# Second MLP of a fused attention and MoE kernel: sums of the next tokens' blocks pinned on VectorE, four low parts moved there from GpSimd

## The chip, the core and the metric

The kernel runs on one core of one Trainium2 chip, in one launch. The metric is the device time of a launch in microseconds (us), lower is better. A time stated for a kernel is the median of several runs.

## The reference, cut to what matters

Attention over packed keys feeds a gated MLP, whose result (4608 tokens by 512) feeds a second MLP. The change touches the second MLP alone:

```python
def _moe2_ref(x, w_in, w_out):               # x 4608x512, w_in 512x2048, w_out 2048x512
    h = x @ w_in
    g = h * (1.0 / (1.0 + np.exp(-1.702 * h)))
    return (g @ w_out).astype(np.float32)
```

## The kernel before, in words

The second MLP starts at about 899 us of the 1638 us span. It reads `x` as the first MLP left it in DRAM.

**Tokens and groups.** Tokens are taken in five spans: three of 2x512 tokens, then two of 2x384. Each span runs four turns (groups of hidden units; `turns` lists span and group). Both matrix products are done on 2x2 blocks with seven products in place of eight, so that sums and differences of blocks are needed: of the tokens (`t1` to `t4`, beside the blocks `b11`, `b12`, `b21`, `b22`), of the hidden values and of the weights. Every factor is split into a high part (rounded by ScalarE) and a low part (the rest, by a subtraction), and each product is three matmuls: high by high, high by low, low by high.

**Steps.** `main` runs a loop over steps `c`. `up(c)` issues six matmuls of a product with the input weights (`ps_up`, L1065) and what reads its bank of PSUM: VectorE adds (L1078, L1080, L1085, L1087) and ScalarE's activation (L1088). A turn has 14 such steps, seven products for each of two halves `a`. `form(d)` makes one of seven factors for the product with the output weights: sums on VectorE (L1101 to L1103, L1105), the high part `oh` on ScalarE (L1109), the low part `ol` on GpSimd (L1110). `down(d)` issues the matmuls (`ps_dn`, L1136) and VectorE's additions to `accu` and `acc` (L1163, L1167). Each `down` uses one of two pairs of PSUM banks in alternation, and each `up` one of four banks, so TensorE waits where VectorE has not yet read a bank that comes round again.

**The next span's tokens.** `load_x` fetches the blocks of the next span, `sums(s, q)` makes their sums on VectorE in three calls: `t1` (L1024), `t3` (L1026) and `t2` (L1030, two instructions). In the program these stand in the span before the one that they serve, at steps 10 and 13 of its third turn and at step 2 of its fourth (`EARLY`). `prepare(s, q)` later splits each block into its two parts (L1041, L1042), in the last half of the fourth turn, and there also subtracts L1045.

**Order.** The program is recorded and a scheduler with a model of the engines' times then picks the order in which each engine's instructions stand. It may put an instruction ahead of others that the program has before it. Each engine then runs its own list strictly in that order. `tc.keep_in_program_order(i)` takes this freedom from one instruction.

Of the kernel before, what the change touches and what calls it, by code (L numbers as in the profile page):

```python
# [26 lines left out]
def fl(t):  # L27

    return t.bitcast(F32)
# [3 lines left out]
def tile_pack_attention__then__two_mlps(  # L33
# [14 lines left out]
    nc = tc.nc  # L48
# [782 lines left out]
    def mlp2(cv):  # L831
# [92 lines left out]
        def load_part(dst, i0, at0, n):  # L924
            end = at0 + n
            while at0 < end:
                b, s0 = divmod(at0, S)
                m = min(end - at0, S - s0)
                o = at0 + n - end
                nc.sync.dma_start(dst[:, :, o : o + m], x2_d[b][:, i0 : i0 + 2, s0 : s0 + m])  # L930
                at0 += m
# [55 lines left out]
        def main(wp, sp, pm, pa, later):  # L987
            turns = [(s, g) for s in range(len(spans)) for g in range(NGR)]
# [15 lines left out]
            xr = {}  # L1004

            def load_x(s):
                if s < len(spans):
                    t0, n = spans[s]
                    for q, i0, k in (("b11", 0, 0), ("b12", 0, 1), ("b22", 2, 1), ("b21", 2, 0)):
# [4 lines left out]
                        xr[q] = t[:, :, :n]  # L1014
                        load_part(xr[q], i0, t0 + k * n, n)

            def sums(s, q):

                if s == len(spans):
                    return  # L1020
                n = spans[s][1]
                if q == "t1":
                    xr[q] = wp.tile([P, 2, TH], F32, tag="xt", name="xr", bufs=1)[:, :, :n]
                    nc.vector.tensor_sub(xr[q], xr["b12"], xr["b11"])  # L1024
                elif q == "t3":
                    nc.vector.tensor_sub(xr["b12"], xr["b22"], xr["b12"])  # L1026
                else:
                    xr[q] = [cv.tile([P, TH], F32, tag="w", name="xr", bufs=2)[:, :n] for _ in range(2)]
                    for k in range(2):
                        nc.vector.tensor_sub(xr[q][k], xr["b22"][:, k], xr["t1"][:, k])  # L1030

            def prepare(s, q):

# [58 lines left out]
            def form(d):  # L1092

                t, j = divmod(d, 7)
                n = spans[turns[t][0]][1]
                a11, a12, a21, a22 = (g[t, z] for z in ((0, 0), (1, 0), (0, 1), (1, 1)))
                q = down_order[j][0]
                if q == "s2":
                    x = sp.tile([P, 2, TH], F32, tag="s1", name="s1", bufs=1)[:, :, :n]
                    g[t, "s1"] = x  # L1100
                    nc.vector.tensor_add(x, a21, a22)  # L1101
                    nc.vector.tensor_sub(a21, a11, a21)
                    nc.vector.tensor_sub(a11, x, a11)  # L1103
                elif q == "s4":
                    nc.vector.tensor_sub(a12, a12, a11)  # L1105
                source = {"a11": a11, "s2": a11, "a12": a12, "s4": a12, "s3": a21, "a22": a22}
                src = g[t, "s1"] if q == "s1" else source[q]
                oh, ol = (sp.tile([P, 2, TH], F32R, tag=f"o{x}", name=f"o{x}", bufs=3)[:, :, :n] for x in "hl")
                nc.scalar.copy(oh, src)  # L1109
                nc.gpsimd.tensor_sub(ol, src, fl(oh))  # L1110
                formed[d] = oh, ol

            acc, banks = {}, {}
# [68 lines left out]
            for d in range(7 * len(turns)):  # L1182
                t, j = divmod(d, 7)
# [3 lines left out]
            for c in range(len(ups) + PER + LAG):  # L1187
                if c < len(ups):
                    up(c)
                    load_wi(c + WIB)  # L1190
                    if c >= 7:
                        next(later, None)
                    s, at = turns[ups[c][0]][0], (turns[ups[c][0]][1] - NGR + 2) * PER + c % PER
                    if at == 6:
                        load_x(s + 1)
                    elif at in EARLY:
                        sums(s + 1, EARLY[at])
                for d in form_at.get(c, ()):
                    form(d)
                for d in down_at.get(c, ()):  # L1200
                    down(d)
                    load_wo(d + WOB)
# [167 lines left out]
```

## Time and profile before

| what | value |
|---|---|
| median of 3 runs | 1644.51 us (1642.76 to 1645.05) |
| the profiled execution | 1639.52 us, its span 1637.7 us |
| TensorE (PE) busy | 1599.6 us, 98% of the span |
| VectorE (DVE) busy | 1098.9 us, 67% |
| GpSimd (POOL) busy | 927.6 us, 57% |
| ScalarE (ACT) busy | 872.0 us, 53% |

The span runs from the first to the last instruction of the core; the profiled execution has 1.8 us around it. PE's busy time is that of matmuls, whose ends are modelled. Below, POOL is GpSimd and DVE is VectorE, as the profile's rows call them.

### The profile page before, as it was taken

The page shows a single profiled execution, that of the slowest core. Times are in us where ns is not written, and L with a number is a line of the kernel's source. Part 1 is how long each engine was busy: PE and PEld are TensorE (multiplying, and loading weights), DVE is VectorE, ACT ScalarE, POOL GpSimd, SP SyncE. Part 2 cuts the span into 40 slices and gives each one's busy share as a digit, 9 for nine tenths or more (in the row PEclk, how much of TensorE's full clock was granted, in tenths as well). Part 3 has the DMA queues.
Part 4 walks back from the last instruction along what each step waited for, and adds up shares of the span by engine and source line. Part 5 has one row for each costly group of instructions (what it writes and reads, how often), then busy time and mean ns, then how long its engine had stood idle before and what let it go on. Part 6 is the DMA issues. An engine that isn't in the chain of part 4 may idle for free.

```text
span 1637.7 us, 29088 instructions
## 1 busy us (share of the span) xinstructions
PE 1599.6 (98%) x10608; PEld 1514.1 (92%) x10608; DVE 1098.9 (67%) x1895; ACT 872.0 (53%) x1799; POOL 927.6 (57%) x753
## 2 busy tenths in 40 slices
PE   8999999999999999999999999899989999999997
PEld 5699999999999999999999899799979999999997
DVE  5777777767777777676764676844584458567466
ACT  5677777666566665565654544344343434434432
POOL 3547877656665566554655475554455445646444
PEclk9999999999999999999999999999999999999999
DMA  9756665866546655484544996576657667887874
GB/s 263 220 170 190 212 203 193 275 198 213 202 161 217 194 170 169 158 309 148 176 172 174 317 326 195 189 242 190 182 189 237 192 191 225 284 252 247 285 232 141
DMA packets 217725, 348.21 MB, mean 213 GB/s; under 512 B 93936, under 2 KB 123632, under 8 KB 211440
## 3 DMA queue, kind: packets, MB, share of 16 engines
q1 hardware_dynamic: 217584, 346.35, 66.0%
q8 instruction: 85, 1.39, 0.4%
q14 instruction: 56, 0.46, 0.1%
HBM read 279.19 MB, written 67.11 MB: 211 GB/s over the span
## 4 chain that ended last, share of the span: by engine, by line
PE 90%; DVE 5%; issue 1%; DMA 1%; ACT 1%; POOL 0%; SPq 0%; POOLq 0%; DVEq 0%; ACTq 0%
PE ps_dn L1136 20%; PE ps_up L1065 19%; PE ps_o L748 19%; PE ps_g L712 18%; PE ps_w L679 4%; PE ps_at L308 3%; PE ps_at L297 3%; PE ps_at L353 2%; PE ps_at L443 2%; DVE xr L1030 1%; PE ps_at L341 1%; DVE x_t L1042 1%; DMA xr<-x 1%; DVE xr L1045 0%; PE ps_at L281 0%
## 5 line engine op out<-in xcount | busy, mean ns | idle before, releaser
L1110 POOL TENSOR_TENSOR ol<-g,oh 128x1024 fp32r<-128x1024 f32 (+1 forms) x120 | 269.4, 2255 | 301.0 <-ACT oh L1109 300.1
L1136 PE MATMUL ps_dn<-wo,oh 128*128 128x256 f32 x2016 | 368.8, 284 | 9.7 <-DVE accu L1163 5.8
L1136 PEld LDWEIGHTS ps_dn<-wo,oh 128*128 128x128 f32 x2016 | 320.5, 192 | 17.4 <-DVE accu L1163 6.2
L748 PE MATMUL ps_o<-Hh,wo 128*128 128x384 f32 x1152 | 320.3, 340 | 0.1
L1136 PE MATMUL ps_dn<-wo,ol 128*128 128x256 f32 x1008 | 280.7, 284 | 1.0 <-POOL ol L1110 1.0
L712 PE MATMUL ps_g<-Aqh,Wh 128*128 128x288 f32 x768 | 231.7, 302 | 3.8 <-DVE th L722 2.7
L712 PE MATMUL ps_g<-Aql,Wh 128*128 128x288 f32 x768 | 226.2, 295 | 0.0
L712 PE MATMUL ps_g<-Aqh,Wl 128*128 128x288 f32 x768 | 226.0, 295 | 0.0
L734 POOL TENSOR_TENSOR Hl<-th,Hh 128x576 fp32r<-128x576 f32 x96 | 138.2, 1440 | 138.0 <-ACT Hh L733 137.8
L1065 PE MATMUL ps_up<-x_t,wi 128*128 128x512 f32 (+1 forms) x936 | 213.4, 368 | 1.1 <-DVE g L1087 1.1
L748 PEld LDWEIGHTS ps_o<-Hh,wo 128*128 128x128 f32 x1152 | 209.9, 188 | 2.1 <-DVE th L725 0.3
L1088 ACT ACTIVATE g<-g 128x512 f32<-128x512 f32 (+1 forms) x120 | 70.6, 590 | 237.5 <-DVE g L1085 130.7
L748 PE MATMUL ps_o<-Hl,wo 128*128 128x384 f32 x576 | 194.2, 337 | 0.0
L1136 PEld LDWEIGHTS ps_dn<-wo,ol 128*128 128x128 f32 x1008 | 191.5, 192 | 2.2 <-POOL ol L1110 1.6
L684 DVE TENSOR_TENSOR Wl<-ps_w,Wh 64x512 fp32r<-64x512 f32 x192 | 131.8, 687 | 81.9 <-ACT Wh L683 78.7
L1065 PEld LDWEIGHTS ps_up<-x_t,wi 128*128 128x128 f32 x936 | 166.3, 188 | 20.9 <-DVE g L1087 1.9
L1065 PE MATMUL ps_up<-x_b,wi 128*128 128x512 f32 (+1 forms) x702 | 165.5, 371 | 5.3 <-DVE g L1080 5.3
L763 POOL TENSOR_TENSOR acc<-acc,add 128x384 f32<-128x384 f32 x135 | 138.6, 1038 | 50.2 <-ACT add L761 48.6
L1109 ACT CAST oh<-g 128x1024 fp32r<-128x1024 f32 (+1 forms) x120 | 113.3, 961 | 94.7 <-PE ps_dn L1136 65.5
L683 ACT CAST Wh<-ps_w 64x512 fp32r<-64x512 f32 x192 | 111.5, 581 | 81.9 <-PE ps_w L679 50.7
L712 PEld LDWEIGHTS ps_g<-Aqh,Wh 128*128 128x128 f32 x768 | 144.2, 188 | 7.7 <-DVE th L722 3.2
L1163 DVE TENSOR_TENSOR acc<-acc,ps_dn 128x512 f32<-128x512 f32 (+1 forms) x160 | 99.6, 630 | 72.3 <-PE ps_dn L1136 68.0
(201 smaller groups left out, 3267.5 us busy)
## 6 DMA issues: line engine op xcount, KB each, us to landing
wo<-wo SPq DMA_DIRECT2D x188, 512.0 KB, 3.9
wi<-wi SPq DMA_DIRECT2D x274, 256.0 KB, 3.7
wg<-wg SPq DMA_DIRECT2D x48, 1024.0 KB, 6.4
raw<-in_moe_w_out_dram SPq DMA_DIRECT2D x28, 512.0 KB, 4.6
wi<-stage SPq DMA_DIRECT2D x24, 512.0 KB, 4.0
wo<-stage SPq DMA_DIRECT2D x24, 512.0 KB, 3.6
x<-acc SPq DMA_DIRECT2D x32, 288.0 KB, 3.3
vn<-in_v_dram SPq DMA_DIRECT2D x16, 512.0 KB, 6.9
```

The lines of the kernel that those rows point to most:

```text
L683: nc.scalar.copy(Wh[rows, :, g], src)
L684: nc.vector.tensor_sub(Wl[rows, :, g], src, fl(Wh[rows, :, g]))
L712: nc.tensor.matmul(ps, st[:, o, g, c * P : (c + 1) * P], mv[:, g, cols], start=n == 0, stop=n == 3 * NG - 1)
L734: nc.gpsimd.tensor_sub(Hl, th, fl(Hh))
L748: nc.tensor.matmul(ps, st[:, m * P : (m + 1) * P], mv[:, cols], start=n == 0, stop=n == 3 * len(ss) - 1)
L763: nc.gpsimd.tensor_add(a, a, t)
L1065: nc.tensor.matmul(o, w[:, y, k], x[:, z, k], start=i == 0 and not go_on, stop=i == 5, skip_group_check=bool(go_on))
L1088: nc.scalar.activation(gf, o if q == "a12" else gf, AF.Gelu_apprx_sigmoid)
L1109: nc.scalar.copy(oh, src)
L1110: nc.gpsimd.tensor_sub(ol, src, fl(oh))
L1136: nc.tensor.matmul(o[:, r], x[:, a, (r0 + r) * P : (r0 + r + 1) * P], w[:, a, y], start=i == 0 and not go_on, stop=i == 6 * m - 1, skip_gr ...
L1163: nc.vector.tensor_add(z, z, o[:, :m])
```

## The change

The five instructions of `sums` that the source writes (twice two for `t2`) keep their place in program order. In the last turn of the last span the low parts of the last four factors (`j` from 3 to 6) are subtracted by VectorE, not GpSimd.

```diff
+            def pinned(i):
+                tc.keep_in_program_order(i)
+
             def sums(s, q):
...
                 if q == "t1":
...
-                    nc.vector.tensor_sub(xr[q], xr["b12"], xr["b11"])
+                    pinned(nc.vector.tensor_sub(xr[q], xr["b12"], xr["b11"]))
                 elif q == "t3":
-                    nc.vector.tensor_sub(xr["b12"], xr["b22"], xr["b12"])
+                    pinned(nc.vector.tensor_sub(xr["b12"], xr["b22"], xr["b12"]))
                 else:
...
                     for k in range(2):
-                        nc.vector.tensor_sub(xr[q][k], xr["b22"][:, k], xr["t1"][:, k])
+                        pinned(nc.vector.tensor_sub(xr[q][k], xr["b22"][:, k], xr["t1"][:, k]))
...
                 nc.scalar.copy(oh, src)
-                nc.gpsimd.tensor_sub(ol, src, fl(oh))
+                late = t == len(turns) - 1 and j >= 3
+                (nc.vector if late else nc.gpsimd).tensor_sub(ol, src, fl(oh))
```

Lines from `sums` on stand three further down in the changed kernel (the sums are L1027, L1029 and L1033, the adds of `up` L1081 to L1090), and from the low part on four (`ol` is L1114, `down`'s additions L1167 and L1171).

Before, VectorE's list around the start of the second span of tokens reads as follows. The L1045 is the last of the second span's own preparation; L1024, L1026 and L1030 are the sums for the third span, a whole span ahead of their place in the program. `s_13422` belongs to the formation of the factors, `accu` and `acc` to `down`.

```order
L1045 TENSOR_TENSOR xr<-xr 128x512
L1024 TENSOR_TENSOR xr<-xr 128x1024
L1087 TENSOR_TENSOR g<-u_13230,ps_up 128x512 x2
L1042 TENSOR_TENSOR x_t_13413<-xr,x_t_13413 128x512 x2
L1163 TENSOR_TENSOR acc_12270<-acc_12270,ps_dn 128x2x256
L1101 TENSOR_TENSOR s_13422<-g 128x1024
L1163 TENSOR_TENSOR acc_12270<-acc_12270,ps_dn 128x2x256
L1102 TENSOR_TENSOR g<-g 128x1024
L1103 TENSOR_TENSOR g<-s_13422,g 128x1024
L1163 TENSOR_TENSOR accu<-accu,ps_dn 128x512 x2
L1026 TENSOR_TENSOR xr<-xr 128x1024
L1030 TENSOR_TENSOR xr<-xr 128x512 x2
```

In the changed kernel these four instructions are gone from that place. They stand at the end of the third turn of the second span (L1027 and L1029) and early in its fourth (L1033), nearly three turns further on. `acc` with its number is one of the two halves of the result in the making, `u` the value that L1081 builds up:

```order
L1027 TENSOR_TENSOR xr<-xr 128x1024
L1167 TENSOR_TENSOR acc_13902<-acc_13902,ps_dn 128x2x256 x2
L1090 TENSOR_TENSOR g<-u_14433,ps_up 128x512 x2
L1029 TENSOR_TENSOR xr<-xr 128x1024
L1104 TENSOR_TENSOR s_14596<-g 128x1024
L1167 TENSOR_TENSOR acc_13903<-acc_13903,ps_dn 128x2x256 x2
L1105 TENSOR_TENSOR g<-g 128x1024
L1106 TENSOR_TENSOR g<-s_14596,g 128x1024
L1167 TENSOR_TENSOR accu<-accu,ps_dn 128x512 x2
L1081 TENSOR_TENSOR u_14643<-u_14643,ps_up 128x512
L1083 TENSOR_TENSOR g<-u_14643,ps_up 128x512
L1033 TENSOR_TENSOR xr<-xr 128x512 x2
```

The same holds for the sums of the fourth and fifth span; those of the second span, which stood near their place already, stand six to fourteen rows later than before. On SyncE's queue a few loads of `x` and of weights change places with their neighbours at the same spots.

At the end of the program VectorE's list in the changed kernel holds the four low parts (L1114) between the additions; that of factor 3 stands four rows ahead of these, those of factors 4 to 6 here. `acc_18516` and `acc_18517` are the two halves of the last result. GpSimd's list ends with the low parts of factors 0 to 2 of that turn.

```order
L1114 TENSOR_TENSOR ol<-g,oh 128x2x384
L1167 TENSOR_TENSOR acc_18516<-acc_18516,ps_dn 128x2x256
L1171 TENSOR_TENSOR acc_18516<-acc_18516,accu 128x3x256
L1171 TENSOR_TENSOR acc_18517<-acc_18517,accu 128x3x256
L1167 TENSOR_TENSOR acc_18516<-acc_18516,ps_dn 128x256
L1114 TENSOR_TENSOR ol<-g,oh 128x2x384
L1167 TENSOR_TENSOR acc_18517<-acc_18517,ps_dn 128x2x256
L1167 TENSOR_TENSOR acc_18517<-acc_18517,ps_dn 128x256
L1114 TENSOR_TENSOR ol<-g,oh 128x2x384
L1171 TENSOR_TENSOR acc_18517<-acc_18517,accu 128x3x256
L1167 TENSOR_TENSOR acc_18516<-acc_18516,ps_dn 128x2x256
L1167 TENSOR_TENSOR acc_18517<-acc_18517,ps_dn 128x2x256
```

L1114 is new in this list. Of the other rows one moved: the addition of factor 5 into `acc_18516` (last row but one) stands ahead of the two additions of factor 4 into `acc_18517`, of which the last row is the first; it stood behind both.

## Rows read from the trace of the kernel before

**Rows 1.** First line of the page: span and instructions.

```profile
span 1637.7 us, 29088 instructions
```

**Rows 2.** Waits, TensorE, 899 to 1609 us: who waited; total, times, longest.

```profile
PE ps_up L1065 <- DVE g L1080: 5.3, 1, 5.3
PE ps_dn L1136 <- DVE accu L1163: 5.0, 1, 5.0
PE ps_dn L1136 <- ACT oh L1109: 1.6, 1, 1.6
PE ps_up L1065 <- DVE g L1087: 1.1, 2, 0.7
```

**Rows 3.** Timeline, 1045 to 1060 us: start, duration, engine, instructions, [idle before <-releaser].

```profile
1047.36 2.32 DVE L1026 TENSOR_TENSOR xr<-xr 128x1024 f32<-128x1024 f32 x1 [1.13 <-DMA xr<-x]
1049.61 5.61 DVE L1030 TENSOR_TENSOR xr<-xr 128x512 f32<-128x512 f32 x2
...
1046.21 5.72 POOL L1110 TENSOR_TENSOR ol<-g,oh 128x1024 fp32r<-128x1024 f32 x2 [7.23 <-ACT oh L1109]
1051.89 2.78 POOL L1110 TENSOR_TENSOR ol<-s,oh 128x1024 fp32r<-128x1024 f32 x1
...
1056.60 2.93 PE L1065 MATMUL ps_up<-x_b,wi 128*128 128x512 f32 x6 [5.29 <-DVE g L1080]
```

**Rows 4.** Timeline, 1213 to 1220 us and 1378 us.

```profile
1213.11 5.34 DVE L1030 TENSOR_TENSOR xr<-xr 128x384 f32<-128x384 f32 x2
...
1219.10 0.80 PE L1136 MATMUL ps_dn<-wo,oh 128*128 128x256 f32 x2 [5.04 <-DVE accu L1163]
...
1378.26 0.74 PE L1136 MATMUL ps_dn<-wo,oh 128*128 128x256 f32 x4 [1.57 <-ACT oh L1109]
```

**Rows 5.** Busy us by stretch: length, PE, PEld, DVE, ACT, POOL; clock, DMA share, GB/s.

```profile
1056.60:1061.60 5.00, 5.00 (x21) 4.42 (x22) 4.00 (x6) 2.20 (x3) 1.86 (x1) 0.61 0.17 44
1219.10:1224.10 5.00, 5.00 (x23) 5.00 (x24) 3.65 (x5) 0.68 (x2) 1.58 (x1) 0.50 0.01 3
1483.00:1523.00 40.00, 40.00 (x287) 40.00 (x286) 31.25 (x48) 17.99 (x34) 26.36 (x16) 1.00 0.80 249
```

**Rows 6.** Timeline, VectorE, TensorE and GpSimd, 980 us and 1156 to 1182 us.

```profile
980.83 1.28 DVE L1030 TENSOR_TENSOR xr<-xr 128x512 f32<-128x512 f32 x2
...
1156.54 0.69 DVE L1163 TENSOR_TENSOR acc<-acc,ps_dn 128x512 f32<-128x512 f32 x1 [2.11 <-PE ps_dn L1136]
1161.33 1.22 DVE L1101 TENSOR_TENSOR s<-g 128x1024 f32<-128x1024 f32 x1
1171.39 0.69 DVE L1080 TENSOR_TENSOR g<-u,ps_up 128x512 f32<-128x512 f32 x1
1172.79 2.60 DVE L1105 TENSOR_TENSOR g<-g 128x1024 f32<-128x1024 f32 x1
...
1173.86 0.28 PE L1136 MATMUL ps_dn<-wo,ol 128*128 128x256 f32 x1
1180.28 1.55 PE L1065 MATMUL ps_up<-x_t,wi 128*128 128x512 f32 x6
...
1156.91 2.41 POOL L1110 TENSOR_TENSOR ol<-g,oh 128x1024 fp32r<-128x1024 f32 x1 [6.71 <-ACT oh L1109]
1167.17 4.77 POOL L1110 TENSOR_TENSOR ol<-g,oh 128x1024 fp32r<-128x1024 f32 x2 [7.86 <-ACT oh L1109]
1171.89 2.42 POOL L1110 TENSOR_TENSOR ol<-s,oh 128x1024 fp32r<-128x1024 f32 x1
```

**Rows 7.** Timeline, VectorE and GpSimd, 1612 to 1629 us.

```profile
1612.60 0.95 DVE L1102 TENSOR_TENSOR g<-g 128x768 f32<-128x768 f32 x1
...
1619.74 2.25 DVE L1105 TENSOR_TENSOR g<-g 128x768 f32<-128x768 f32 x1
...
1622.85 4.17 DVE L1167 TENSOR_TENSOR acc<-acc,accu 128x768 f32<-128x768 f32 x2
...
1621.14 7.58 POOL L1110 TENSOR_TENSOR ol<-g,oh 128x768 fp32r<-128x768 f32 x3
```

## The prediction, written before the changed kernel ran

> **What bounds the kernel now.** The page comes first: the profiled execution took 1639.52 us, of which the span is 1637.7 us [rows 1], and TensorE is busy for nearly all of it. So the time is TensorE's work plus the places where it stands still, and the next view to read is that of TensorE's waits from the start of the second MLP to the last turn. It is short [rows 2]: one wait of 5.3 us for L1080, one of 5.0 us for the additions to `accu`, one of 1.6 us for the high parts, and two for L1087, 1.1 us together. VectorE stands behind all four; the high parts are ScalarE's, but they are made from VectorE's L1103.
>
> The timeline around these waits shows what VectorE did instead. In the first place it stands 1.13 us for the arrival of the next but one span's tokens, then L1026 takes 2.32 us and the two L1030 5.61 us; only after them come L1078 and L1080, and TensorE starts again at 1056.60, after 5.29 us [rows 3]. In the second place the pair L1030 takes 5.34 us, and TensorE starts at 1219.10 after 5.04 us [rows 4]. In the third the high parts come 1.57 us late [rows 4]; L1026 and L1030 stand ahead of L1103 there. These are the three starts of a span (second, third and fourth) at which VectorE's list before holds the sums for the span after.
>
> The stops cost more than their length. In the 5 us after the first, the granted clock is 0.61, after the second 0.50, where it is 1.00 in an undisturbed stretch [rows 5]. Of the two levels, 1.2 and 2.4 GHz, TensorE had the lower one for all of the 5 us after the second stop and most of those after the first. At full busy time the loss is (1 - 0.61) x 5 = 1.95 us and (1 - 0.50) x 5 = 2.5 us.
>
> **What the change takes away.** The sums leave these three places altogether. The waits are 5.3 + 5.0 + 1.6 + 1.1 = 13.0 us, the clock 1.95 + 2.5 = 4.45 us, together 17.45 us. That nothing else holds the start of a span is read from the fourth such start, of the fifth span: there no sums stand in the list, the preparation does, and the 40 us from 1483 are busy throughout, at clock 1.00 [rows 5].
>
> **What it adds there.** The sums still run, the same instructions, at the end of the third turn and in the fourth of the same span. I look at the place in the second span where they go. `t1` comes after L1085 and ahead of an addition for which VectorE idles 2.11 us; alone, a subtraction of this shape takes 1.22 us, and GpSimd is idle for 6.71 us up to 1156.91, so it lies in a hole: nothing [rows 6]. `t3` goes ahead of L1101 and pushes L1101 to L1103, and through them the high and low parts of the new turn, back by about 1.2 us. GpSimd's run of three low parts then starts 1.2 us after 1167.17 [rows 6]. The first of them takes half of the run's 4.77 us and is ready near 1170.8; TensorE, which has factor 0 (formed before these sums) and three products to do first, takes up a low part at 1173.86 [rows 6]. So this too costs nothing.
>
> `t2` is the doubtful one. It stands after L1080, which ends at 1172.1, and by then GpSimd is in its run of three, to about 1174.3 before and 1175.5 now [rows 6]. Alone the pair takes 1.28 us [rows 6]; within such a run it took 5.61 us [rows 3], since each half sat out one of GpSimd's instructions. Those are the bounds, and I take the upper one, as the place has the same run beside it: VectorE is free again at 1172.1 + 5.6 = 1177.7, about 4 us later than before. What queues behind it: L1085, then L1105, which already takes 2.60 us here for the same reason without TensorE stopping, and the additions to `accu`. For whom: L1085 frees the bank of the last product of this half, whose six matmuls begin at 1180.28 [rows 6]; L1085, done at 1177.7 + 0.7 = 1178.4, is 2 us early. The product before it needs L1080, which stands ahead of the pair. So: nothing at the places with 512 columns. In the fourth span, with 384 columns, each step is a quarter shorter and the margin with it; I put 0.5 us there. The bounds for all places: nothing, and 5.3 + 1.95 = 7.2 us each, the first place's whole price.
>
> The Trainium skill's page "SBUF — State Buffer", section "Who interferes with whom", says that a VectorE instruction with two inputs in SBUF and a GpSimd instruction that reads SBUF exclude each other for the whole instruction, and the one that starts first goes first. The trace agrees (5.61 us against 1.28 us for the same pair). By that rule alone `t2` would be as slow in its new place as in the old, which speaks against a gain there; the sum by it is the same as long as TensorE's margin holds, and the rival "slower" if it doesn't.
>
> The loads of `x` keep their places to within a few entries of SyncE's queue and so arrive where they did, nearly three turns ahead of the sums; only the second span's sums are near their loads, and they move away from them. No wait for a transfer is left.
>
> **The end of the program.** In the last turn GpSimd's low parts collide with VectorE's sums: L1105 takes 2.25 us and two L1167 4.17 us, where the same shape alone takes 0.95 us [rows 7]. Of these, 1.3 + 2.3 = 3.6 us are waiting. GpSimd's run of the last three low parts, 7.58 us [rows 7], goes away, and with it the waiting; but VectorE gets 4 x 0.95 = 3.8 us of work. The first of the four can run in the idle time while TensorE does factor 1, and one addition now stands ahead of the two that the last product waits for, by about 0.6 us. What remains is 3.8 - 0.95 + 0.6 - 3.6, about nothing: I take a gain of 0.4 us. The bounds are a gain of 3.6 us (all four hidden) and a loss of 3.8 us (no waiting saved).
>
> The Trainium skill's "Perfetto Trace Analysis", section "Optimizing Scalar/DVE Operations", warns that moving operations between VectorE and GpSimd might not help, as they share a way into SBUF. By that the end gains nothing at all and the sum is 17.0 us, not 17.4.
>
> **The sum.** 17.45 - 0.5 + 0.4 = 17.35 us. The span goes from 1637.7 to 1620.3 us and the profiled execution from 1639.52 to 1622.2 us. The median of the runs is 5 us above the profiled execution; I take the same 17.4 us off it: 1644.5 - 17.4 = 1627.1, so 1627 us.
>
> **Rivals.**
> The sums cost half in their new places. The pair `t2` sits out GpSimd's low parts at four places, and if TensorE's margin is smaller than I read it, each gives back up to one such instruction, 2.8 us. For it: the pair's 5.6 us are as likely there. Against it: the 2 us that I count between L1085 and its product. Time: 4 x 2.8 = 11.2 us back, 1638 us. Chance 0.10.
>
> The start of the span is the cause, not the sums. L1042 and L1045 of the preparation crowd VectorE there as well, and with the sums gone TensorE could wait for the next late thing, L1101 to L1103. For it: the third wait names the high parts. Against it: the fifth span's start. Time: about 1644 us. Chance 0.05.
>
> Slower. By the exclusion that the rows show, the pinned pair holds VectorE's list at each of four places, three of which had no stop before, as long as it did in the first place: 4 x 7.2 = 28.8 us against 17.45 us taken away, 1656 us. It decides from 17.45 / 4 = 4.4 us a place. Against it: what was late in the first place, L1080, stands ahead of the pair in the new one. Chance 0.05.
>
> **How the numbers follow.** The forecast has 0.80, its own range 1622 to 1631 us: the end of the program's bounds either way. The range for 8 times in 10 also takes in most of the half-cost case: 1621 to 1636 us. A measurement of this kernel can tell about 0.2%, 3.3 us, from no change. Faster by more than that: forecast and half cost, 0.90. Within it: the second rival, 0.05. Slower: 0.05.
>
> **What the changed profile would show.** Right: no TensorE wait above 1 us between 899 us and the last turn; clock 1.00 throughout that stretch; the L1027, L1029 and L1033 in the third and fourth turns, L1033 at 1.3 to 5.6 us a pair; the matmuls' number as before; the end within a few us of the same length. Wrong: new waits of TensorE named after L1088, L1108 or `accu` in the early fourth turns, a clock below 1.00 behind them, or VectorE waiting for a load of `x`. A tail that is longer by more than 2 us would show VectorE's last list without a gap.

## The result, and the profile after

The changed kernel takes 1619.51 us (median of 4 runs, 1617.48 to 1620.15), the kernel before beside it 1643.63 us (4 runs, 1641.84 to 1645.05): a ratio of 0.9852, 95% interval 0.9835 to 0.9869. That is 24.1 us off, where 17.4 were predicted; 1627 us was forecast, with 1621 as the lower end of the range. In a second set of runs, beside others of before (median 1642.75 us), the changed kernel took 1618.94 us, ratio 0.9860 (0.9846 to 0.9874). The median of its eight runs is 1619.2 us.

The page of the changed kernel begins with its span; [rows 1] had 1637.7 us.

```profile
span 1618.2 us, 29102 instructions
```

TensorE's waits from 899 to 1570 us (who waited for whom: total, times, longest), then windows (length; busy us of PE, PEld, DVE, ACT, POOL; clock, DMA share, GB/s):

```profile
PE ps_up L1068 <- issue: 0.7, 1, 0.7
PE ps_dn L1140 <- POOL ol L1114: 0.4, 1, 0.4
```

```profile
1040.00:1060.00 20.00, 20.00 (x133) 18.36 (x133) 15.29 (x19) 7.80 (x10) 12.05 (x6) 1.00 0.77 237
1200.00:1225.00 25.00, 25.00 (x158) 22.57 (x157) 15.35 (x20) 8.85 (x11) 19.65 (x9) 1.00 0.71 218
1300.00:1400.00 100.00, 100.00 (x683) 95.56 (x682) 69.03 (x89) 41.82 (x65) 56.44 (x28) 1.00 0.74 239
```

All four lines of [rows 2] are gone, and the three starts of a span are busy throughout at clock 1.00, where [rows 5] had 0.61 and 0.50. The sums stand where the prediction put them (for each span `sums` issues four instructions: one for `t1`, one for `t3`, two for `t2`); the timeline of VectorE and GpSimd in the second span, which answers to [rows 6]:

```profile
1145.97 1.22 DVE L1027 TENSOR_TENSOR xr<-xr 128x1024 f32<-128x1024 f32 x1
1152.95 1.22 DVE L1029 TENSOR_TENSOR xr<-xr 128x1024 f32<-128x1024 f32 x1
1163.62 4.62 DVE L1033 TENSOR_TENSOR xr<-xr 128x512 f32<-128x512 f32 x2
1168.16 0.67 DVE L1088 TENSOR_TENSOR g<-g,ps_up 128x512 f32<-128x512 f32 x1
...
1160.12 4.77 POOL L1114 TENSOR_TENSOR ol<-g,oh 128x1024 fp32r<-128x1024 f32 x2 [9.18 <-ACT oh L1112]
1164.85 2.84 POOL L1114 TENSOR_TENSOR ol<-s,oh 128x1024 fp32r<-128x1024 f32 x1
```

The pair takes 4.62 us beside GpSimd's run, nearly as long as in its old place (5.61 us, [rows 3]). There the same length stopped TensorE; here nothing that TensorE needs soon stands behind it.

**Where the time came from.** ScalarE copies the bank of the first product of each half of a turn into `u`, 40 times in the second MLP (L1076, L1079 in the changed kernel), and the copies follow TensorE closely. The start of the same copy in two profiles shows between which of them time was gained. The table takes the 4th, 11th, 19th and 40th copy (940.45, 1077.52, 1234.92 and 1578.84 us in the second profile of the changed kernel, the base) and gives what each kernel needs more than the base from one to the next; the last column is from the 40th copy to the end of the span. The names of kernels are explained below.

| profile | span | 1st place | 2nd place | 3rd place | 40th copy to end |
|---|---|---|---|---|---|
| predicted, by place | | 8.0 | 7.9 | 1.6 | 0.4 less |
| before | 1637.7 | 9.1 | 8.3 | 2.0 | 39.8 |
| before again (e1) | 1639.9 | 9.8 | 10.0 | 1.9 | 39.8 |
| late parts only (e3) | 1639.5 | 9.8 | 8.6 | 1.7 | 38.7 |
| after | 1618.2 | 0.7 | 0.0 | 0.0 | 39.0 |
| after again (a2), base | 1617.5 | 0 | 0 | 0 | 38.7 |
| sums pinned only (e2) | 1620.4 | 0.3 | 0.0 | 0.0 | 39.9 |

The row of the prediction is its 17.45 us by place: 5.3 + 1.95 + 0.7 for the first, 5.0 + 2.5 + 0.4 for the second (0.7 and 0.4 being L1087's two waits, [rows 2]), 1.6 for the third. In the profile on which the sum was made the three places cost 9.1 + 8.3 + 2.0 = 19.4 us; in the second profile of the same kernel 21.7 us, and in e3, which has the same stops, 20.1 us. The 0.7 and 0.3 us of after and e2 in the first column were lost before 1000 us, ahead of the place.

### The profile page after: what moved, and what is told of

Same layout as the page of the kernel before. It is cut to its first block, busy times and chain, and to the rows that moved or that the text cites. A ratio compares the mean times of both kernels' runs of the same rounds, so it can differ in the third digit from the quotient of the medians.

```text
span 1618.2 us, 29102 instructions
## 1 busy us (share of the span) xinstructions
PE 1593.0 (98%) x10608; PEld 1510.4 (93%) x10608; DVE 1094.5 (68%) x1899; ACT 870.6 (54%) x1799; POOL 915.7 (57%) x749
## 4 chain that ended last, share of the span: by engine, by line
PE 90%; DMA 2%; DVE 2%; ACT 2%; issue 2%; POOL 1%; SPq 0%; POOLq 0%; DVEq 0%; ACTq 0%
PE ps_dn L1140 21%; PE ps_up L1068 20%; PE ps_o L748 18%; PE ps_g L712 18%; PE ps_w L679 4%; PE ps_at L308 3%; PE ps_at L297 2%; PE ps_at L353 2%; PE ps_at L443 2%; DMA kw<-in_k_dram 1%; DMA vn<-in_v_dram 1%; POOL ol L1114 1%; PE ps_at L341 0%; DMA raw<-in_moe_w_out_dram 0%; DVE Wl L684 0%
## 5 line engine op out<-in xcount | busy, mean ns | idle before, releaser
L1114 POOL TENSOR_TENSOR ol<-g,oh 128x1024 fp32r<-128x1024 f32 (+1 forms) x117 | 258.9, 2223 | 295.7 <-ACT oh L1112 292.9
L1167 DVE TENSOR_TENSOR acc<-acc,ps_dn 128x512 f32<-128x512 f32 (+1 forms) x160 | 99.0, 630 | 71.9 <-PE ps_dn L1140 62.1
```

What stands on the lines that cost most here:

```text
L1114: (nc.vector if late else nc.gpsimd).tensor_sub(ol, src, fl(oh))
L1167: nc.vector.tensor_add(z, z, o[:, :m])
```

## The theories and the experiments

Three theories were set against each other. **A**: the stops cost more in most executions than in the profiled one. **B**: the profiled execution of before was short elsewhere, and the stops cost what was read. **C**: the missing time lies in the end of the program. Later **R** says how the price can vary: the load of `x` and ScalarE's high parts race, VectorE's sum or GpSimd's low part starts first, and the other sits it out.

### e1: the kernel before, again

> The kernel before, unchanged, looked at again. The sum was made in a profiled execution of 1639.5 us, while its timed runs lay at 1641.8 to 1645.1 us; the changed kernel's profiled execution (1620.0 us) lies among its own. Theory A (the stops in the three places cost more in most executions than in the profiled one): the new profile lies near 1643 us, and the 3 to 5 us that it is longer than the first are found between 899 and 1610 us, as longer waits of TensorE behind the sums or a lower or longer low clock behind them; the first 899 us are equal within 1 us. Rival B (the first profile was short elsewhere: loads at the start, the clock in the first layers, or the tail): the extra microseconds lie outside 899 to 1610 us, and the four stops still cost 13.0 us of wait and 4.5 us of clock.

1641.23 us (11 runs, 1639.66 to 1645.47) beside 1641.69 us (23 runs, 1638.40 to 1647.87) of the same program: before spreads over 9.5 us. The new profile (1641.73 us) is 2.2 us longer than the first, up to the 4th copy 0.1 us shorter, and its end is equal; the whole difference is in the first and second place. That is A, though less than the 3 to 5 us that it expected, and between these two profiles nothing is left for B. The second place in the first profile:

```profile
1212.24 0.96 DVE L1026 TENSOR_TENSOR xr<-xr 128x768 f32<-128x768 f32 x1 [0.39 <-DMA xr<-x]
...
1212.41 5.63 POOL L1110 TENSOR_TENSOR ol<-g,oh 128x1024 fp32r<-128x1024 f32 x2 [7.21 <-ACT oh L1109]
```

and in the second, with the two 5 us windows behind the stops:

```profile
1213.35 2.84 DVE L1026 TENSOR_TENSOR xr<-xr 128x768 f32<-128x768 f32 x1 [0.93 <-DMA xr<-x]
1216.11 5.30 DVE L1030 TENSOR_TENSOR xr<-xr 128x384 f32<-128x384 f32 x2
...
1212.98 5.40 POOL L1110 TENSOR_TENSOR ol<-g,oh 128x1024 fp32r<-128x1024 f32 x2 [7.21 <-ACT oh L1109]
...
1222.06 0.79 PE L1136 MATMUL ps_dn<-wo,oh 128*128 128x256 f32 x2 [7.45 <-DVE accu L1163]
```

```profile
1056.42:1061.42 5.00, 5.00 (x17) 4.44 (x18) 3.61 (x5) 2.19 (x3) 1.85 (x1) 0.50 0.13 43
1222.06:1227.06 5.00, 5.00 (x25) 4.91 (x26) 4.09 (x6) 1.13 (x2) 0.00 (x0) 0.63 0.01 3
```

TensorE waits 7.45 us instead of 5.04 ([rows 4]), because L1026 takes 2.84 us instead of 0.96: its load landed 0.93 us after VectorE was ready (0.39 in the first profile), and GpSimd had begun 0.37 us earlier, where in the first profile it began 0.17 us later. The clock differs too: 0.50 instead of 0.61 behind the first stop, 0.63 instead of 0.50 behind the second ([rows 5]). 2.4 us more wait and 0.65 us less clock make the 1.7 us of the second place; 0.55 us more clock nearly the 0.7 us of the first, whose wait is 5.29 us in both. In the first place the clock fell earlier in the first profile: over the last 2 us of the stop, in which TensorE did next to nothing, it is 0.50 in the first profile and 0.68 in the second.

```profile
1054.60:1056.60 2.00, 0.01 (x1) 0.01 (x1) 1.91 (x3) 0.00 (x0) 0.07 (x1) 0.50 0.00 0
```

```profile
1054.42:1056.42 2.00, 0.00 (x0) 0.00 (x0) 1.91 (x3) 0.00 (x0) 0.08 (x1) 0.68 0.00 0
```

So a stop of one length costs more or less, as the low clock falls on the stop or on the work behind it. e3 shows the same wait once more, with 0.65 before its end and 0.50 in the 5 us behind.

### e2 and e3: the two parts of the change, each alone

```diff
-                late = t == len(turns) - 1 and j >= 3
+                late = False                              # e2
```

```diff
             def pinned(i):
-                tc.keep_in_program_order(i)
+                pass                                      # e3
```

> One part of the change alone: the sums stay in program order, and all low parts of the last group stay on GpSimd. Prediction's sum: the sums are worth 17.0 us, the tail 0.4 us. Theory A: the pinned sums hold nearly all of the 24 us, so this kernel is 23 to 24 us below the kernel before and within 1 us of the changed kernel. Rival C (the tail's low parts hold what the sum missed): this kernel is only 17 to 19 us below the kernel before, 5 to 7 us above the changed one, and its profile shows the stretch behind the last up projection 5 us longer.

> The other part alone: the sums are free as before and fall to the first places again; the last four low parts go to VectorE. Theory A: 0.4 to 1 us below the kernel before (the stretch behind the last up projection was 27.3 us before and 26.5 us after in the two profiles), that is hardly to be told from it; TensorE's four waits (about 5.3, 5.0, 1.6, 1.1 us) and the low clock behind two of them are back. Rival C: 5 to 7 us below the kernel before.

e2: 1621.39 us (4 runs, 1620.41 to 1622.41), ratio 0.9867 (0.9849 to 0.9886) to before: 20.3 us below it, between what A and C had said. e3: 1639.91 us (12 runs), ratio 0.9990 (0.9977 to 1.0003), not told from before. In the profiles the end is shorter by 1.1 to 1.2 us where the four low parts are on VectorE (38.7 in e3 and a2 against 39.8 and 39.9 us; 39.0, so 0.8 us, in the first profile of the changed kernel, which had a low clock there), and the places are free wherever the sums are pinned. Of the 2.2 us by which e2 lies above the changed kernel the end is 1.2; another 1.4 us its profile has more than a2's up to the 4th copy. So the pinned sums carry nearly all. C falls: it wanted e3 5 to 7 us below before and the end of e2 5 us longer; still, the tail is worth two to three times the 0.4 us predicted. Up to the 4th copy e3's profile is 2.2 us longer than the first of before (942.32 against 940.08 us), so a part of the spread lies outside the stops, as B has it.

### e4 and e5: the sums of one span free again

```diff
+                    if s != 2:                            # e4; s != 3 in e5
                         tc.keep_in_program_order(i)
```

`pinned` stands inside `sums` here, where the span `s` is known.

> The changed kernel with the sums of one span (the third) free, so that they alone fall back to their first place, where the kernel before waited 5.0 us and ran 2.5 us at the low clock behind it. By the prediction's terms this gives back 7.5 us: 1627.1 us where the changed kernel has 1619.6. Theory A (a stop costs a third more than in the profiled execution): it gives back 9 to 11 us. Rival B (the missing microseconds were no part of the stops): 7 to 8 us. Should the wait not come back although the sums are at the old place, then place alone isn't the cause, and it gives back less than 1 us.

> The changed kernel with the sums of the fourth span alone left free: they fall back to the second place, in the order that the kernel before has there. Two profiles of the kernel before show this stop with 5.04 and 7.45 us of wait: the load of x landed 0.39 and 0.93 us after VectorE was ready for it, and the first sum, starting just ahead of GpSimd's low parts or just behind the first of them, took 0.96 or 2.84 us. Theory R (this race between the load and ScalarE's high parts sets the price): it gives back 7.5 to 10 us, 1627 to 1630 us, and its own runs lie in two heaps some 2 to 3 us apart or spread by 3 us or more, where the kernel with only the third span's sums free had its four runs within 0.8 us. Rival (the varying part lies elsewhere): runs within 1.5 us of each other, at one of the two prices.

The first expectation names the terms of the second place by mistake; those of the first are 5.3 + 1.95 = 7.25 us. e4 takes 1625.44 us (4 runs, 1624.74 to 1625.52), 6.3 us above the changed kernel. The first column of the table would be 6.1 us for its profile, but 1.1 of these were lost before 1000 us, so the place cost 5.0 us: less than either theory's figure. The order around the sums isn't quite that of before (the second addition to `accu` stands behind them), and TensorE waits twice for little, in place of once for 5.29 us, with clock 0.67 in the 5.24 us from the first restart to the second:

```profile
1046.63 1.21 DVE L1030 TENSOR_TENSOR xr<-xr 128x1024 f32<-128x1024 f32 x1
...
1047.27 5.57 POOL L1115 TENSOR_TENSOR ol<-g,oh 128x1024 fp32r<-128x1024 f32 x2 [6.92 <-ACT oh L1113]
...
1050.12 0.38 PE L1141 MATMUL ps_dn<-wo,ol 128*128 128x256 f32 x1 [1.42 <-POOL ol L1115]
1055.36 1.67 PE L1069 MATMUL ps_up<-x_b,wi 128*128 128x512 f32 x6 [1.30 <-DVE g L1084]
```

```profile
1050.12:1055.36 5.24, 3.94 (x20) 3.64 (x21) 5.15 (x5) 0.00 (x0) 5.24 (x2) 0.67 0.31 96
```

`t3` (here L1030) waits for no load and starts 0.64 us ahead of GpSimd: 1.21 us instead of the 2.32 us of [rows 3]. So e4 shows that the sums bring a stop back, but not the whole price of the first place. e5 takes 1629.53 us (5 runs), 10.3 us above the changed kernel, and its runs spread over 3.8 us (1627.42 to 1631.25) where e4's lie within 0.8: as R has it, the second place varies. Its first profile was its shortest run, with a load 0.19 us late, `t3` at 0.96 us and a wait of 4.87 us, and cost 7.6 us there:

```profile
1203.52 0.96 DVE L1030 TENSOR_TENSOR xr<-xr 128x768 f32<-128x768 f32 x1 [0.19 <-DMA xr<-x]
...
1203.90 5.43 POOL L1115 TENSOR_TENSOR ol<-g,oh 128x1024 fp32r<-128x1024 f32 x2 [7.22 <-ACT oh L1113]
...
1210.40 0.80 PE L1141 MATMUL ps_dn<-wo,oh 128*128 128x256 f32 x2 [4.87 <-DVE accu L1168]
```

A second profile of the same kernel, e10, caught a long run.

> The kernel with the sums of the fourth span free, one more look: its five runs lay at 1627.4 to 1631.3 us, and its profile was of the lowest (load 0.19 us late, t3 0.96 us, TensorE's wait 4.87 us). Theory R: a run near 1630 us shows t3 at 2.8 us behind a GpSimd low part and a wait of about 7 us; a run near 1627.5 us shows the profile as before. Rival: the same t3 and wait, and 2 to 3 us more at the low clock.

It took 1632.70 us, and the second place cost 10.5 us (`t3` is L1030 again):

```profile
1206.43 3.07 DVE L1030 TENSOR_TENSOR xr<-xr 128x768 f32<-128x768 f32 x1 [0.70 <-DMA xr<-x]
...
1206.30 5.40 POOL L1115 TENSOR_TENSOR ol<-g,oh 128x1024 fp32r<-128x1024 f32 x2 [7.22 <-ACT oh L1113]
...
1215.38 0.80 PE L1141 MATMUL ps_dn<-wo,oh 128*128 128x256 f32 x2 [7.45 <-DVE accu L1168]
```

The load comes 0.5 us later than in the first profile, `t3` starts 0.13 us behind GpSimd's low part instead of 0.38 us ahead of it, and TensorE waits 2.6 us longer.

### e6, e8, e9: only `t3` pinned

`t1` and the pair `t2` are free, and `t2` returns without `t3` to the first and the second place. It returns to the third as well, which costs 1.7 to 1.9 us again in the three profiles.

```diff
-                    pinned(nc.vector.tensor_sub(xr[q], xr["b12"], xr["b11"]))
+                    nc.vector.tensor_sub(xr[q], xr["b12"], xr["b11"])
...
-                        pinned(nc.vector.tensor_sub(xr[q][k], xr["b22"][:, k], xr["t1"][:, k]))
+                        nc.vector.tensor_sub(xr[q][k], xr["b22"][:, k], xr["t1"][:, k])
```

> The changed kernel with only the sum that waits for the load (t3) in program order; t1 and the pair t2 are free, and t2 stands alone in the first and the second place, between the two additions to accu. Theory R: with the load's wait and the 0.96 to 2.84 us of t3 gone, t2 starts ahead of GpSimd's low parts, its first half takes under 1 us and its second sits out one low part: 3 to 4 us for the pair instead of 5.3 to 5.6. The waits shrink to under 2 us at each of the two places and the low clock behind them to 0 to 2.5 us: 2 to 7 us above the changed kernel in all, 1621.5 to 1626.5 us, with runs within 3 us. Rival (the pair alone makes the stop, the load matters little): TensorE's waits stay near 5 us at both places and the kernel lies 14 us or more above the changed one, beyond 1633 us.

> The kernel with only t3 in program order, unchanged, one more look: its six runs lay in two heaps, 1626.5 and 1627.8 us, and four at 1631.3 to 1631.6 us, and its profile was of the lowest. There the pair t2 took 1.28 us in the first place (it started 0.65 us ahead of GpSimd's low parts) and 3.21 us in the second (0.15 us ahead of them, after 0.42 us of waiting for the load). Theory R (who starts first sets the price): a run of the upper heap shows a pair of 5.3 to 5.6 us in the first or the second place, started behind the first of GpSimd's low parts, and a wait of TensorE of 4 to 5.5 us there; a run of the lower heap shows none. Rival (the heaps are two lengths of the low clock): pairs and waits are the same in both heaps, and only the time at the low clock differs by 4 to 5 us.

> The same kernel once more, so that a run of either heap is likely to be seen; the same expectations.

The six runs of e6 are in two groups: 1626.50 and 1627.80 us, and 1631.28 to 1631.61 us (median 1631.30). The lower group lies at the upper end of what R had expected or 1.3 us beyond it, the upper group 5 us beyond it: the expectation overlooked that `t2` reads the same load (`b22`) and so keeps the race, and that the third place comes back. The two further profiles fell into the two groups, e8 at 1625.95 and e9 at 1631.09 us. In both, the first place costs 1.4 us or less (the pair starts 0.6 us ahead of GpSimd, takes 1.28 us, and TensorE waits 0.16 us); the second place costs 3.2 us in e8 and 7.8 us in e9. There, e8:

```profile
1204.71 3.22 DVE L1033 TENSOR_TENSOR xr<-xr 128x384 f32<-128x384 f32 x2 [0.25 <-DMA xr<-x]
...
1205.03 5.13 POOL L1114 TENSOR_TENSOR ol<-g,oh 128x1024 fp32r<-128x1024 f32 x2 [7.21 <-ACT oh L1112]
...
1208.58 0.50 PE L1140 MATMUL ps_dn<-wo,oh 128*128 128x256 f32 x2 [1.89 <-DVE accu L1167]
```

```profile
1208.58:1213.58 5.00, 4.90 (x31) 4.36 (x32) 4.86 (x5) 1.74 (x3) 3.95 (x2) 1.00 0.06 20
```

and e9, again with the window behind the stop:

```profile
1205.66 5.29 DVE L1033 TENSOR_TENSOR xr<-xr 128x384 f32<-128x384 f32 x2 [0.69 <-DMA xr<-x]
...
1205.54 5.00 POOL L1114 TENSOR_TENSOR ol<-g,oh 128x1024 fp32r<-128x1024 f32 x2 [7.22 <-ACT oh L1112]
...
1211.60 0.80 PE L1140 MATMUL ps_dn<-wo,oh 128*128 128x256 f32 x2 [4.43 <-DVE accu L1167]
```

```profile
1211.60:1216.60 5.00, 5.00 (x17) 4.42 (x18) 3.05 (x4) 1.11 (x2) 1.57 (x1) 0.50 0.01 3
```

One program, two times. A load that lands 0.44 us later puts the pair 0.12 us behind GpSimd instead of 0.32 us ahead; its first half then sits out a low part too (5.29 instead of 3.22 us), TensorE waits 2.5 us longer, and its clock falls to 0.50, where it stays 1.00 in the 5 us behind e8's wait. The two terms, 2.5 us each, make 5.0 us, where the copies show 4.6 us more in that place. The rival, that the groups differ in the low clock alone, falls: pairs and waits differ as well.

### a2 and e7: the changed kernel again, and two more low parts on VectorE

```diff
-                late = t == len(turns) - 1 and j >= 3
+                late = t == len(turns) - 1 and j >= 1     # e7
```

> The changed kernel, unchanged, looked at again beside the three kernels below on one chip. Its profiled execution had one low clock of its own, in the tail behind two short waits of TensorE (0.89 and 0.43 us), where a group of two matmuls took 0.63 instead of 0.40 us; its four runs lay at 1617.5 to 1620.2 us. Theory A (the stops of the kernel before cost a varying price, the changed kernel has no stop that long): runs within about 3 us, 1617 to 1620.5 us, median near 1619.5 us, no wait of TensorE over 1 us up to the last turn. Rival: the changed kernel's runs vary as those of before do (9.5 us over 23 runs), and the four were lucky.

> The changed kernel with two more low parts of the last turn on VectorE, six instead of four; GpSimd then has none beside VectorE in the tail. In the profile of the changed kernel GpSimd's two take 4.33 us there, TensorE waits 0.43 us for the first of them, and VectorE's own low part beside them takes 1.22 instead of 0.95 us; VectorE has holes of 1.5 and 1.5 us there. If sitting each other out is the cost: 0.4 to 1.2 us faster, 1618.3 to 1619.1 us. If VectorE's list is full instead: 0.5 to 1.5 us slower.

a2 ran within 2.7 us (1617.48 to 1620.22), and so do all eight runs of the changed kernel, where the 23 runs of before spread over 9.5 us: without the stops most of the spread is gone, as A has it. How much of it R makes isn't shown. Each run's granted clock is on record, and over the 23 runs it goes from 0.996 in the shortest to 0.992 in the longest, which is (0.996 - 0.992) x 1640 = 6.6 us of the 9.5, an estimate from figures with three decimals; the changed kernel has 0.998 to 1.000. By this estimate much of the long runs' excess is time at the low clock. No profile caught a run of before above 1641.73 us.

e7 takes 1618.45 us (4 runs, 1618.35 to 1619.48); its median is 0.5 us below a2's 1618.94 and by time alone the two aren't told apart, but from the 40th copy to the end it needs 37.45 us instead of 38.66. The waits of TensorE in that end, a2:

```profile
1596.70 1.47 PE L1140 MATMUL ps_dn<-wo,oh 128*128 128x256 f32 x8 [0.89 <-ACT oh L1112]
1598.61 0.39 PE L1140 MATMUL ps_dn<-wo,ol 128*128 128x256 f32 x1 [0.44 <-POOL ol L1114]
1601.11 0.39 PE L1140 MATMUL ps_dn<-wo,ol 128*128 128x256 f32 x1 [0.57 <-POOL ol L1114]
1610.76 0.47 PE L1140 MATMUL ps_dn<-wo,oh 128*128 128x256 f32 x2 [0.88 <-issue]
```

and e7:

```profile
1597.01 1.47 PE L1140 MATMUL ps_dn<-wo,oh 128*128 128x256 f32 x8 [0.89 <-ACT oh L1112]
1606.59 0.48 PE L1140 MATMUL ps_dn<-wo,oh 128*128 128x256 f32 x2 [0.44 <-issue]
1609.85 0.47 PE L1140 MATMUL ps_dn<-wo,oh 128*128 128x256 f32 x2 [0.88 <-issue]
```

With only factor 0's low part left to GpSimd in the last turn, the two waits for its low parts go, and one of 0.44 us comes that waits for nothing the profile shows. Its median is the lowest of this study.

## Why the prediction was right, and where it failed

**The mechanism was right.** The sums at the three places made the stops (e2 without them, e4 to e6 with some of them back), the low clock came with the two long stops, and pinning the sums took both away.

**The step that failed** is the last of the sum: "The median of the runs is 5 us above the profiled execution; I take the same 17.4 us off it". It treats the stops' price as fixed and their 17.45 us as true of any run. Three things were wrong with it.

First, 17.45 us was too small even for the profiled execution, where the places cost 19.4 us. [rows 2] leaves out one line of its own view, a wait for GpSimd's low part in the first place:

```profile
PE ps_dn L1136 <- POOL ol L1110: 0.6, 1, 0.6
```

The other 1.4 us weren't settled.

Second, the price changes between executions: 19.4, 21.7 and 20.1 us in the three profiles that have all the stops. The profiled execution had the cheap outcome of the race at the second place; the second profile, which lies at the median of the 23 runs beside it, had the dear one. e3's had the cheap one and more low clock. By medians, e2 against before, the sums are worth 20.3 us.

Third, the 5 us between profile and median are not all the stops' doing. They rest on a median of three runs, 1644.51 us; larger sets of the same kernel have 1642.75 (11 runs) and 1641.69 us (23 runs), 3.2 and 2.2 us above the profile. That a median stood above the profile could still have been read as a sign that the price varies. The forecast's own range had no room for that: its width is said to be the tail's bounds, and those give 1624 us as the lower end, not the 1622 that is written.

Of the 7.5 us between 1627 and 1619.5, the stops' price is 2 to 4 us, the median of three runs 2 to 3, the tail and the new places 1.3.

**The new places** were put at 0.5 us, all of it for the span with 384 columns. They cost nothing that stands out: the copies of after run level with those of a2 from the 11th on, the pairs there took 4.61, 4.62, 4.08 and 3.72 us, inside the bounds, and TensorE's margin behind L1088 held. So neither the rival "half the cost" nor "slower" came in, though the pair was nearly as slow as they supposed. The rival "start of the span" fell with e2.

**The tail** was mis-sized: 1.2 us (0.8 in the changed kernel's first profile) against 0.4. The prediction's own terms give 0.15 us, and the step from there to 0.4 has no reason. The waiting went as read: L1108 (L1105 before) takes 0.96 us and the two L1171 1.82 us in a2, where [rows 7] has 2.25 and 4.17. TensorE's waits of 0.77 and 1.41 us are gone; one of 0.88 us is new, in a2 also one of 0.57 us.

```profile
1622.38 0.51 PE L1136 MATMUL ps_dn<-wo,oh 128*128 128x256 f32 x2 [0.77 <-DVE accu L1163]
1627.40 0.50 PE L1136 MATMUL ps_dn<-wo,oh 128*128 128x256 f32 x2 [1.41 <-DVE acc L1163]
```

```profile
1601.09 0.96 DVE L1108 TENSOR_TENSOR g<-g 128x768 f32<-128x768 f32 x1 [0.30 <-POOL ol L1114]
1603.77 1.82 DVE L1171 TENSOR_TENSOR acc<-acc,accu 128x768 f32<-128x768 f32 x2
```

That more of the four subtractions fell into VectorE's gaps than the estimate allowed is likely; it wasn't measured one by one. The Trainium skill's "Perfetto Trace Analysis", section "Optimizing Scalar/DVE Operations", says that offloading between GpSimd and VectorE might not help. Here it did, in the profiles: four subtractions moved gave 1.2 us, two more another 1.2 us (38.66 to 37.45).

With these, 19.4 to 21.7 us for the stops and 1.2 for the tail, the sum is 20.6 to 22.9 us. The medians of before in the three sets (1643.63, 1642.75, 1641.69) lie 24.4, 23.6 and 22.5 us above the changed kernel's 1619.2: the upper end of the sum reaches the largest set, the one with 23 runs. What the two smaller sets have beyond it stays open.

## What to carry to other kernels

A stop whose length depends on which of two engines starts first has no single price: before summing from one profile, ask which outcome it caught, and take a spread of the kernel's own runs, or a median above the profile, as a hint that it caught the cheap one. Read the clock inside the stop as well as behind it. Where VectorE's two-input work and GpSimd share a stretch, what stands behind the slow instruction decides its cost, not its length: 4.6 us cost nothing in the new place and over 5 us of wait in the old.

## What was not expected of the hardware

A load of `x` that landed 0.44 us later made the second place 4.6 us longer (e8, e9), and one that landed 0.5 us later 2.8 us longer (e5, e10). Ahead of GpSimd by 0.65 or 0.32 us, or behind it by 0.12 us, the pair took 1.28, 3.22 and 5.29 us (the first with 512, the others with 384 columns). The Trainium skill's "SBUF — State Buffer", section "Who interferes with whom", says that a VectorE instruction with two inputs in SBUF contends with a GpSimd instruction that reads SBUF, and that the order of issue decides who blocks; the trace agrees with these three figures.

Short waits were followed by the low clock in one execution and not in another. In the third place of before the 5 us behind a wait of 1.57 us have clock 1.00, in e4 the 3 us from 1051, behind a wait of 1.42 us, have 0.50. Behind the same two waits in the tail (0.89 and 0.43 or 0.44 us) the changed kernel's first profile has clock 0.83, its second 1.00. The 10 us from 1597, first profile and then second:

```profile
1597.00:1607.00 10.00, 9.49 (x62) 9.09 (x63) 7.03 (x11) 3.92 (x6) 4.33 (x2) 0.83 0.52 152
```

```profile
1597.00:1607.00 10.00, 8.99 (x71) 8.38 (x70) 7.82 (x11) 3.62 (x5) 4.06 (x2) 1.00 0.49 156
```

Why it falls in the one and not in the other wasn't settled. The low clock explains the first profile's longer end, 39.0 instead of 38.7 us, in part at least.
